# Fourier mixing and a long convolution on one core: u and K side by side in one tile of the second transform stage

## Chip, cores and metric

The kernel runs on one core of one Trainium2 chip. The metric is the time of one execution on the device in microseconds, the median of several runs. A profile of one further execution shows what each engine did.

## What is computed

The output has two halves side by side. The first is a Fourier mixing layer on x (2048 x 512) with given real and imaginary matrices. The second is a state-space layer: a kernel K of 2048 taps for each of 512 channels is built from exponentials, u (2048 x 512) is convolved with it by transforms of length 4096, and u times a skip factor is added.

```python
# first half
a = einsum("bsd,ed->bse", x, dft_hid_re)
b = einsum("bsd,ed->bse", x, dft_hid_im)
y = einsum("ts,bse->bte", dft_seq_re, a) - einsum("ts,bse->bte", dft_seq_im, b)
# second half
P = exp((A * dt[:, None])[:, :, None] * pos[None, None, :])
K = 2.0 * einsum("dn,dnl->dl", C, P).real
Kf, Uf = rfft(K, 2 * L), rfft(u_t, 2 * L)
y = irfft(Uf * Kf[None], 2 * L)[:, :, :L]
y = y.transpose(0, 2, 1) + u * D_skip
```

## The kernel before

Two programs share the engines. `Fnet` does the first half: twelve groups of outputs, each made of four accumulators of 128 x 512, and every step of a group multiplies three products of split operands (high times high, high times low, low times high) in `matmuls`, line 304. These 1,920 matmuls are the stream that fills TensorE. Its operands are loaded into `raw` (line 272, on SP's queue) and split by ScalarE (line 184) and VectorE (line 188) into `hi` and `lo`; four `raw` buffers and three split pairs are in turn.

`Ssm` does the second half in pieces that are put in between. `tables1` and `tables2` build factors of the exponentials on VectorE and ScalarE (lines 543 to 572). `taps` (line 739) multiplies two such tables into the taps of K for 32 channels, 16 times. `stage1_k` (line 769) and `stage1_u` (line 812) do the first stage of the transform, of K eight times and of u eight times, and store the result in device memory (`xk`, `xu`). `product` does the rest for one of 16 groups: four parts h of 128 channels by four ranges q of frequencies. It multiplies the first-stage result of u and of K by the second-stage pieces `w2` (line 890), copies both spectra from the accumulator banks with ScalarE (line 903), multiplies them on VectorE (lines 906 to 919), and applies the first piece of the inverse (line 926) into `zs`. `inverse` (line 972) ends a part.

The order of all instructions is fixed before the run: generators yield an engine and an estimated duration, an event or a semaphore of buffers, and the class `Plan` simulates them and writes the instructions out in the order in which they would start. Each engine then works through its own list in that order. Almost all loads and stores are issued by one queue, SP's.

The load of one group's first-stage result is `load_spectrum`: two DMAs, for r = 0 and 1, from line 863, into a tile `xt_u` for u and another, `xt_k`, for K, of 128 x 2 x 4 x 128 floats each. The two names have counts of free buffers, `b.xts["u"]` and `b.xts["k"]`: one buffer for the parts h = 0 to 2, two for h = 3. `spectra` runs once for u and once for K, waits for a buffer and spawns the load. `products` waits for both loads, takes two pairs of accumulator banks and spawns `product`. In it, r, then u or K, then the real or imaginary output c, then the strip xx of 32 output rows and the half g of the contracted rows are looped over, one matmul each:

```python
nc.tensor.matmul(got[r][1][32 * xx:32 * xx + 32, g, o:o + PART],
                 self.w2[rows, 2 * q + r, xx, 32 * c:32 * c + 32], xt[rows, r, xx],
                 start=True, stop=True, tile_position=(64 * g, 32 * xx))
```

A matmul contracts 64 rows into 32 outputs for 128 columns, and takes one of eight tiles of the array (two by row, four by column). All operands are 32-bit floats; `PART` is 128. In one accumulator bank lie, 128 columns each, u real, u imaginary, K real and K imaginary.

Early in the run, before any spectrum is loaded, `stage1_u` uses the same two buffers for its inputs: piece k of u goes to `xt_u` for even k and to `xt_k` for odd k (line 806).

Of the kernel before, what the change touches and what calls it, by code (L numbers as in the profile page):

```python
# [8 lines left out]
F32 = mybir.dt.float32  # L9
# [7 lines left out]
SEQ, DM, NS = 2048, 512, 128  # L17
PART = DM // 4
# [127 lines left out]
def act(cols):  # L146
    return 0.09 + cols * 0.00085


def dve(cols, rate=1.0):  # L150
    return (62 + cols / rate) / 960


def load(kb):
    return max(0.55, kb / 330)
# [210 lines left out]
class Ssm:  # L366
# [423 lines left out]
    def spectrum_u(self):  # L790

        self.uleft = 16
        yield self.const_ev
        b = self.sets[0]
        yield b.zls
        self.xu_sb, self.xus = b.pool.tile([128, 2, 2, DM], F32, name="zl", bufs=b.n), Sem(2)
        for k in range(8):
            name = "uk"[k % 2]
            yield self.sets[0].xts[name]
            self.plan.spawn(self.stage1_u(k, name), 1)  # L800

    def stage1_u(self, k, name):
        nc, b = self.nc, self.sets[0]
        u = b.pool.tile([128, 2, DM], F32, name=f"xt_{name}")
        yield "dma", load(512)
        nc.sync.dma_start(u, self.uG[:, 2 * k:2 * k + 2])
        got = yield from self.banks(2)
        yield "pe", 1.82
        for m in range(2):
            for r in range(2):  # L810
                rows = slice(64 * r, 64 * r + 64)
                nc.tensor.matmul(got[m][1][:, r], self.f1u[rows], u[rows, m], start=True, stop=True,  # L812
                                 tile_position=(64 * r, 0))
        self.plan.put(b.xts[name])
        for m in range(2):
            n = 2 * k + m
            sem = b.zbs if n % 3 == 2 else self.xus
            yield sem
            x = b.pool.tile([128, 2, DM], F32, name="z", bufs=b.n) if n % 3 == 2 else self.xu_sb[:, n % 3]
            for r in range(2):  # L820
                yield "act", act(512)
                nc.scalar.activation(x[:, r], got[m][1][:, r], AF.Copy)
            self.give(got[m][0])
            self.plan.spawn(self.store_u(x, 2 * k + m, sem), 1)
# [32 lines left out]
                self.plan.spawn(self.load_spectrum(b, name, h, q, view), 1)  # L857

    def load_spectrum(self, b, name, h, q, view):
        xt = self.xt[name, h, q] = b.pool.tile([128, 2, 4, PART], F32, name=f"xt_{name}", bufs=b.n)  # L860
        yield "dma", load(512)
        for r in range(2):
            self.nc.sync.dma_start(xt[:, r], view[2 * q + r])
        self.plan.set(self.xt_ev[name, h, q])

    def products(self):
# [12 lines left out]
    def product(self, b, h, q, got, done):  # L879
        nc, v, a = self.nc, self.nc.vector, self.nc.scalar  # L880
        uk = b.pool.tile([128, 2, 2, 2, 2, PART], F32, name="uk", bufs=b.n)
        yield "pe", 1.86
        for r in range(2):
            for n, name in enumerate("uk"):
                xt = self.xt[name, h, q]
                for c in range(2):
                    for xx in range(4):
                        for g in range(2):
                            rows, o = slice(64 * g, 64 * g + 64), (2 * n + c) * PART
                            nc.tensor.matmul(got[r][1][32 * xx:32 * xx + 32, g, o:o + PART],  # L890
                                             self.w2[rows, 2 * q + r, xx, 32 * c:32 * c + 32], xt[rows, r, xx],
                                             start=True, stop=True, tile_position=(64 * g, 32 * xx))
        for name in "uk":
            self.plan.put(b.xts[name])
        self.plan.set(done)
        u, t = uk[:, :, :, 0], uk[:, :, :, 1]
        yield b.zbs
        P = b.pool.tile([128, 2, 2, 2, PART], F32, name="z", bufs=b.n)
        left, ready = [2], Event()

        def half(r, k, p):
            yield "act", act(1024)
            a.activation(uk[:, r].rearrange("p g n c d -> p g (n c d)"), p, AF.Copy)  # L903
            self.give(k)
            yield "dve", dve(512)
            v.tensor_tensor(P[:, r], t[:, r], u[:, r], op=OP.mult)  # L906
            yield "dve", dve(512), *APART
            v.tensor_tensor(t[:, r], t[:, r], u[:, r, :, ::-1], op=OP.mult)  # L908
            left[0] -= 1
            if not left[0]:  # L910
                self.plan.set(ready)
        for r in range(2):
            self.plan.spawn(half(r, *got[r]), 1)
        yield ready
        yield "dve", dve(512)
        v.tensor_tensor(u[:, :, :, 0], P[:, :, :, 0], P[:, :, :, 1], op=OP.subtract)
        self.plan.put(b.zbs)
        yield "dve", dve(512), *APART
        v.tensor_tensor(t[:, :, :, 0], t[:, :, :, 0], t[:, :, :, 1], op=OP.add)

        def run(got):
            for c, Y in enumerate((u, t)):
                for g in range(2):
                    for xx in range(4):
                        rows = slice(32 * xx, 32 * xx + 32)
                        nc.tensor.matmul(got[xx // 2][1][64 * g:64 * g + 64, xx % 2, :2 * PART], self.ia[rows, c],  # L926
                                         Y[rows, :, g, 0], start=c == 0, stop=c == 1, tile_position=(32 * xx, 64 * g))
        w = Joined(self, run)
        if self.taps_left:
            self.waiting.append(w)  # L930
            yield w
        if w.got is None:
            got = yield from self.banks(2)
            yield "pe", 0.95
            w.run(got, False)
        self.plan.put(b.uks)
        yield b.zbs
        z = b.pool.tile([128, 2, 4, PART], F32, name="z", bufs=b.n)
        for n, (k, p) in enumerate(w.got):
            yield "act", act(512)  # L940
            a.activation(z[:, :, 2 * n:2 * n + 2].rearrange("p r x d -> p x r d"),  # L941
                         p[:, :, :2 * PART].rearrange("p x (r d) -> p x r d", r=2), AF.Copy)
            w.leave(k)
        view = self.zs[h].rearrange("(q x g) c l d -> q (g c l) x d", q=8, x=4)
        yield "dma", load(512)
        for r in range(2):
            nc.sync.dma_start(view[2 * q + r], z[:, r])
        self.plan.put(b.zbs)
        self.left[h] -= 1
        if not self.left[h]:  # L950
            self.plan.set(self.zs_ev[h])
# [108 lines left out]
```

## Time and profile before

| what | us |
|---|---|
| median of 3 runs | 593.32 (591.82 to 596.59) |
| the profiled execution | 595.39 |
| its span, from the first instruction to the last | 593.6 |
| granted TensorE clock in it, share of full speed | 0.997 |

The profile counts each float32 matmul of the second half as two records and each matmul of the stream as one; each record has a weight load (PEld) of its own, which may overlap matmuls. A group row gives line, engine, operation, output and inputs, shapes and count, then busy time and the mean of one in ns, then the idle time of the engine before it and what ended that. The chain of waits is followed back from the last instruction to whatever released each step; "issue" in it is time in which the engine waited for nothing that the profile shows. In a listing by tile, a row has shortest/median/longest duration in ns and the first and last start in us, then the tile of the array (rows*columns) and the moving operand. In a list of waits the three numbers are us in total, times and the longest. A row of a DMA queue has packets, MB and share of the 16 engines' time; a row of DMA issues has the count, KB of each and median us to landing.

### The profile page before, as it was taken

What the parts mean: (1) busy time and instruction counts of PE and PEld (TensorE: products, weight loads), DVE (VectorE), ACT (ScalarE), POOL (GpSimd) and SP (SyncE); (2) the same over time, 40 slices, a digit from 0 to 9 for tenths busy, and PEclk for the clock granted to TensorE, in tenths of its full rate; (3) what the DMA queues carried; (4) which work ended last, traced back from release to release, by engine and by line L of the source; (5) the groups of instructions that cost most, each with busy time, mean ns of one, the idle gap of its engine ahead of it and who ended that gap; (6) DMA issues with size and microseconds to landing.
All of it is one profiled execution on the core that took longest, in us unless ns stands there. A gap on an engine that the chain in (4) does not pass through costs nothing.

```text
span 593.6 us, 16944 instructions
## 1 busy us (share of the span) xinstructions
PE 583.3 (98%) x6982; PEld 451.1 (76%) x6982; DVE 496.6 (84%) x883; ACT 382.2 (64%) x745; POOL 4.6 (1%) x12
## 2 busy tenths in 40 slices
PE   8999999999999999999899999999999999999997
PEld 6767668778788777876687788778776877877785
DVE  7977989999999999999899999999999944245420
ACT  5789884947586587758474876677764635353622
POOL 0000000000000000000000000000000000000000
PEclk9999999999999999999899999999999999999999
DMA  8999996363493359456947783569787744998674
GB/s 270 332 365 334 319 337 198 107 178 94 122 274 100 105 162 280 118 150 174 253 130 228 196 258 116 146 159 287 232 275 209 239 118 144 282 340 267 197 249 142
DMA packets 141247, 125.97 MB, mean 212 GB/s; under 512 B 46193, under 2 KB 106353, under 8 KB 140913
## 3 DMA queue, kind: packets, MB, share of 16 engines
q1 hardware_dynamic: 140880, 124.48, 69.0%
q8 instruction: 55, 0.90, 0.6%
q10 hardware_dynamic: 288, 0.39, 0.2%
q14 instruction: 24, 0.19, 0.1%
HBM read 82.12 MB, written 42.73 MB: 210 GB/s over the span
## 4 chain that ended last, share of the span: by engine, by line
PE 85%; DVE 6%; DMA 3%; issue 2%; ACT 2%; SPq 1%; DVEq 0%; ACTq 0%
PE acc L304 66%; PE f L739 5%; PE f L890 4%; PE f L926 3%; PE f L812 3%; PE f L769 2%; PE f L972 2%; DVE prod L543 2%; DMA zl<-zs 1%; DVE lo L188 1%; DVE t L552 1%; DMA par<-par_dram 1%; DMA uk<-in_x 1%; ACT hi L184 0%; ACT y L327 0%
## 5 line engine op out<-in xcount | busy, mean ns | idle before, releaser
L304 PE MATMUL acc<-hi,x_hi 128*128 128x512 f32 x640 | 257.7, 403 | 0.4 <-ACT x_hi L184 0.2
L304 PE MATMUL acc<-hi,x_lo 128*128 128x512 f32 x640 | 250.6, 392 | 0.3 <-issue 0.2
L304 PE MATMUL acc<-lo,x_hi 128*128 128x512 f32 x640 | 250.5, 391 | 0.2 <-DVE lo L188 0.2
L543 DVE TENSOR_TENSOR prod<-t,cs 128x1024 f32<-128x1024 f32 (+4 forms) x192 | 163.5, 870 | 3.1 <-ACT t L681 0.9
L188 DVE TENSOR_TENSOR lo<-raw,hi 128x512 fp32r<-128x512 f32 x160 | 109.1, 686 | 62.0 <-ACT hi L184 56.2
L184 ACT ACTIVATE hi<-raw 128x512 fp32r<-128x512 f32 x160 | 100.5, 629 | 92.4 <-PE acc L304 68.7
L304 PEld LDWEIGHTS acc<-hi,x_hi 128*128 128x128 f32 x640 | 120.5, 188 | 45.4 <-issue 17.8
L304 PEld LDWEIGHTS acc<-hi,x_lo 128*128 128x128 f32 x640 | 120.7, 189 | 27.1 <-issue 0.7
L304 PEld LDWEIGHTS acc<-lo,x_hi 128*128 128x128 f32 x640 | 120.6, 189 | 24.0 <-DVE lo L188 0.9
L552 DVE TENSOR_TENSOR t<-prod 128x512 f32<-128x512 f32 (+4 forms) x192 | 94.5, 512 | 1.1
L559 ACT ACTIVATE square<-t 128x256 f32<-128x256 f32 (+1 forms) x64 | 36.6, 571 | 21.6 <-DVE t L552 20.2
L327 ACT ACTIVATE y<-acc 128x512 f32<-128x512 f32 x47 | 27.9, 596 | 13.1 <-PE acc L304 9.6
L739 PEld LDWEIGHTS f<-t,t 128*32 128x32 f32 x2048 | 29.5, 110 | 8.0 <-issue 5.7
L903 ACT ACTIVATE uk<-f 128x1024 f32<-128x1024 f32 x32 | 32.1, 1016 | 4.9 <-PE f L890 3.6
L739 PE MATMUL f<-t,t 128*32 128x64 f32 x2048 | 32.4, 220 | 1.7 <-issue 1.7
L906 DVE TENSOR_TENSOR z<-uk 128x512 f32<-128x512 f32 x32 | 22.0, 686 | 8.4 <-ACT uk L903 4.7
L572 DVE TENSOR_TENSOR t<-square 128x128 f32<-128x128 f32 (+1 forms) x64 | 24.7, 386 | 0.3 <-ACT square L559 0.3
L941 ACT ACTIVATE z<-f 128x512 f32<-128x512 f32 x32 | 17.6, 596 | 11.3 <-PE f L739 5.8
L890 PE MATMUL f<-xt_k,w 64*32 64x128 f32 x1024 | 22.7, 271 | 1.9 <-issue 1.9
L618 ACT ACTIVATE cs<-cs 128x352 f32<-128x352 f32 x32 | 15.9, 537 | 11.7 <-DVE cs L613 11.7
L908 DVE TENSOR_TENSOR uk<-uk 128x512 f32<-128x512 f32 x32 | 22.1, 690 | 0.8
L566 DVE SCALAR_TENSOR_TENSOR t<-t 128x128 f32<-128x128 f32 (+2 forms) x48 | 22.4, 466 | 0.4
(85 smaller groups left out, 440.7 us busy)
## 6 DMA issues: line engine op xcount, KB each, us to landing
raw<-in_sT SPq DMA_DIRECT2D x127, 256.0 KB, 3.4
p<-y SPq DMA_DIRECT2D x32, 256.0 KB, 3.9
xt_u<-xu SPq DMA_DIRECT2D x32, 256.0 KB, 5.1
xk<-xk_sb SPq DMA_DIRECT2D x32, 256.0 KB, 4.0
xt_k<-xk SPq DMA_DIRECT2D x32, 256.0 KB, 5.5
zs<-z SPq DMA_DIRECT2D x32, 256.0 KB, 3.7
zl<-zs SPq DMA_DIRECT2D x16, 512.0 KB, 6.3
raw<-p SPq DMA_DIRECT2D x32, 256.0 KB, 4.2
```

The source lines that it names most:

```text
L184: self.nc.scalar.activation(hi, src, AF.Copy)
L188: self.nc.vector.tensor_tensor(lo, src, hi.bitcast(F32), op=OP.subtract)
L304: nc.tensor.matmul(acc[d], l[:, cols], r, start=k == 0 and n == 0, stop=k == len(items) - 1 and n == 2)
L327: self.nc.scalar.activation(y, ps, AF.Copy, scale=-1.0 if g[2] == 1 else 1.0)
L543: self.nc.vector.tensor_tensor(p.rearrange("p k d c m -> p k (d c) m"), src.rearrange("p d c l -> p (d c) l")[:, None, :, rows].to_broadca ...
L552: self.nc.vector.tensor_tensor(dst[:, :, :, rows], p[:, 0], p[:, 1, :, ::-1], op=OP.add)
L559: self.nc.scalar.activation(sq, t[:, :, :, m // 2:m], AF.Square)
L566: self.nc.vector.scalar_tensor_tensor(t[:, :, 1, m:2 * m:2], t[:, :, 0, m // 2:m], 2.0, t[:, :, 1, m // 2:m], op0=OP.mult, op1=OP.mult)
L572: self.nc.vector.tensor_tensor(t[:, :, 0, m:2 * m:2], box[0][:, :, 0], box[0][:, :, 1], op=OP.subtract)
L739: nc.tensor.matmul(ps[32 * j:32 * j + 32, i], t1[:, d, c], t2[:, d, c], start=c == 0, stop=c == 1, tile_position=(0, 32 * j))
L890: nc.tensor.matmul(got[r][1][32 * xx:32 * xx + 32, g, o:o + PART], self.w2[rows, 2 * q + r, xx, 32 * c:32 * c + 32], xt[rows, r, xx], star ...
L903: a.activation(uk[:, r].rearrange("p g n c d -> p g (n c d)"), p, AF.Copy)
```

## The change

The two tiles become one, `xt`, of 128 x 2 x 4 x 2 x 128 floats: for each r and strip xx, the 128 columns of u and next to them the 128 of K. The first of the two loads of a group takes the tile, and each load fills its own 128 columns of every 256. `product` loses the loop over u and K: one matmul takes 256 columns, and its output goes to two strips of the bank, 128 columns apart, so that the bank holds the same as before. The two counts of free buffers stay. `stage1_u` uses the two halves of one such tile for even and odd k. The estimate for the planner, 1.86 us for a product, is not changed.

```diff
         for k in range(8):
             name = "uk"[k % 2]
-            yield self.sets[0].xts[name]
+            yield b.xts[name]
+            if not k:
+                self.u_sb = b.pool.tile([128, 2, 2, DM], F32, name="xt", bufs=b.n)
             self.plan.spawn(self.stage1_u(k, name), 1)
...
-        u = b.pool.tile([128, 2, DM], F32, name=f"xt_{name}")
+        u = self.u_sb[:, k % 2]
...
     def load_spectrum(self, b, name, h, q, view):
-        xt = self.xt[name, h, q] = b.pool.tile([128, 2, 4, PART], F32, name=f"xt_{name}", bufs=b.n)
+        if (h, q) not in self.xt:
+            self.xt[h, q] = b.pool.tile([128, 2, 4, 2, PART], F32, name="xt", bufs=b.n)
+        xt = self.xt[h, q]
         yield "dma", load(512)
         for r in range(2):
-            self.nc.sync.dma_start(xt[:, r], view[2 * q + r])
+            self.nc.sync.dma_start(xt[:, r, :, "uk".index(name)], view[2 * q + r])
...
+        xt = self.xt[h, q]
         for r in range(2):
-            for n, name in enumerate("uk"):
-                xt = self.xt[name, h, q]
-                for c in range(2):
-                    for xx in range(4):
-                        for g in range(2):
-                            rows, o = slice(64 * g, 64 * g + 64), (2 * n + c) * PART
-                            nc.tensor.matmul(got[r][1][32 * xx:32 * xx + 32, g, o:o + PART],
-                                             self.w2[rows, 2 * q + r, xx, 32 * c:32 * c + 32], xt[rows, r, xx],
-                                             start=True, stop=True, tile_position=(64 * g, 32 * xx))
+            for c in range(2):
+                for xx in range(4):
+                    for g in range(2):
+                        rows = slice(64 * g, 64 * g + 64)
+                        both = got[r][1][32 * xx:32 * xx + 32, g].rearrange("p (n c d) -> p n c d", n=2, c=2)
+                        nc.tensor.matmul(both[:, :, c], self.w2[rows, 2 * q + r, xx, 32 * c:32 * c + 32],
+                                         xt[rows, r, xx], start=True, stop=True, tile_position=(64 * g, 32 * xx))
```

## The prediction

> **What bounds the kernel now.** I read the page first: shares of the engines, then the chain of waits.
>
> ```profile
> span 593.6 us, 16944 instructions
> PE 583.3 (98%) x6982; PEld 451.1 (76%) x6982; DVE 496.6 (84%) x883; ACT 382.2 (64%) x745; POOL 4.6 (1%) x12
> PE 85%; DVE 6%; DMA 3%; issue 2%; ACT 2%; SPq 1%; DVEq 0%; ACTq 0%
> PE acc L304 66%; PE f L739 5%; PE f L890 4%; PE f L926 3%; PE f L812 3%; PE f L769 2%; PE f L972 2%; DVE prod L543 2%; DMA zl<-zs 1%; DVE lo L188 1%; DVE t L552 1%; DMA par<-par_dram 1%; DMA uk<-in_x 1%; ACT hi L184 0%; ACT y L327 0%
> ```
>
> TensorE is busy 98% of the span and carries 85% of the chain. Two thirds of the chain is the stream of the first part (L304), which the change leaves alone. The transform that changes is L890, 4%. So the question is what one block at L890 costs, and what ends around it.
>
> The merged chain shows each block with its time (start, us, what) and the group rows show how many records a block has.
>
> ```profile
> 27.97 1.92 PE f L812 x8
> 83.17 1.92 PE f L739 x128
> 105.71 1.93 PE f L769 x16
> 169.87 1.96 PE f L890 x128
> 303.48 1.90 PE f L972 x32
> 535.87 1.05 PE f L926 x32
> ...
> L890 PE MATMUL f<-xt_u,w x1024: 267/269/295, 169.8 to 556.2; 64*32 64x128 f32 x171
> L890 PE MATMUL f<-xt_k,w x1024: 268/269/293, 170.3 to 556.6; 64*32 64x128 f32 x171
> L926 PE MATMUL f<-uk,ia x512: 374/374/426, 198.6 to 563.9; 32*64 32x256 f32 x171
> L739 PE MATMUL f<-t,t x2048: 219/219/244, 83.1 to 485.2; 128*32 128x64 f32 x187
> ```
>
> A product has 64 calls of matmul in the code and 128 records in its block: each float32 matmul is two records. With 2,048 records at L890, there are 16 such blocks.
>
> **Does a block pay for instructions or for columns?** Give each record a weight: its columns times the share of the 128x128 array that its tile takes. L890: 128 records x 128 columns x (64x32)/(128x128) = 2,048. L739: 128 x 64 x 1/4 = 2,048. L926: 32 x 256 x 1/8 = 1,024. By their forms in the listing below, L812 (64x128 tiles), L769 (32x128) and L972 (128x64) come to 8 x 512 x 1/2, 16 x 512 x 1/4 and 32 x 128 x 1/2: 2,048 each.
>
> ```profile
> L972 PE MATMUL f<-zl,ib x256: 272/273/323, 303.4 to 583.2; 128*64 128x128 f32 x128
> L769 PE MATMUL f<-ks,f1k x128: 587/587/692, 105.6 to 498.0; 32*128 32x512 f32 x128
> L812 PE MATMUL f<-xt_u,f1u x32: 589/589/693, 27.9 to 74.8; 64*128 64x512 f32 x32
> ```
>
> Every block of weight 2,048 takes 1.90 to 1.96 us, whether it has 8 records or 128; the one of weight 1,024 takes 1.05. So a block costs about 0.85 ns per unit of weight ((1.92 - 1.05)/1,024) and 0.18 us for its ends. It pays for columns, and the tiles side by side are already full.
>
> **Term 1, the block itself.** The change makes it 64 records of 256 columns on 64x32 tiles: 64 x 256 x 1/8 = 2,048, as before. Its nearest row is L926, which is already 256 columns wide, eight tiles in turn: doubling its inner part gives 1.05 + 0.87 = 1.92 us; L972 allows 1.90. So a block gains 0.04 to 0.06 us, about what the narrow form loses to its many weight loads. I take 0.05: 16 x 0.05 = 0.8 us. On the chain L890 has 4.4% of 593.6 = 26 us, some 13 of 16 blocks, so 0.6 to 0.7 us reach the end. I take 0.6, with 0 and 1.0 as ends.
>
> A rule of the Trainium skill would make much more of it: TensorEngine Tiling (Array Packing), section Instruction Overhead, gives each matmul about 60 cycles of overhead, so that one of 1 column takes as long as one of 60. At the 2.4 GHz of its page TensorE: Matmul & The Clock Gate that is an estimated 25 ns, 1.6 us for the 64 records saved in a block, 26 us over 16 blocks. This trace disagrees, as 128 records end in 1.96 us, 15 ns each, and 8 records take 1.92.
>
> **Term 2, the supply of instructions.** "issue" in the chain is time in which nothing shown was awaited. Three such pieces lie inside TensorE's blocks:
>
> ```profile
> 287.86 1.93 PE f L890 x125
> 289.79 1.92 issue
> 291.70 0.41 PE f L890 x3
> ...
> 456.80 1.70 PE f L739 x112
> 458.50 1.07 issue
> ...
> 482.58 1.91 PE f L739 x123
> 484.48 0.62 issue
> ```
>
> Together 1.92 + 1.07 + 0.62 = 3.6 us. TensorE stops near the end of a block whose other records run at full pace. The queues show what runs then; the first row is for the whole span, the others for 289.0 to 291.7, 456.8 to 459.6 and 482.4 to 485.1 us.
>
> ```profile
> q8 instruction: 55, 0.90, 0.6%
> ...
> q8 instruction: 1, 0.02, 2.1%
> ...
> q8 instruction: 1, 0.02, 2.1%
> ...
> q8 instruction: 1, 0.02, 2.8%
> ```
>
> 0.90 MB in 55 packets is 16.4 KB each. TensorE's 2 x 6,982 records over 55 are 254 per packet, so this queue feeds TensorE some 256 instructions at a time. Each stop has one such packet in it, and each comes in a stretch where an inverse piece (32 records and as many weight loads, 64 instructions), a block of taps (256), four pieces of the stream (24) and a product (256) run through 600 instructions in some 8 us. I read the stops as TensorE running out of instructions.
>
> The Trainium skill has the same blocks (Runtime: NRT & Kernel Launch, section Instruction fetch mechanics: 16 KiB, 256 instructions) and says that the fetch is mostly hidden. The size agrees with 16.4 KB; that it is hidden does not fit the three stops here. By that rule term 2 would be nothing, and the forecast 592.7.
>
> The change takes 64 matmul records and 64 weight loads out of every product: 2,048 instructions, 8 packets of 55, and the run of 600 becomes 470. The stop inside L890 (1.92) should go. The two in L739 come before the product, and depend on where the 256 boundary falls; it moves by half a packet with each product, so they may go, stay or turn up elsewhere. I count half: 0.85. Sum 2.8 us, ends 0 (all come back) and 3.6 (all go). What replaces a stop: the stream goes on at once, as L304 has lost nearly nothing to its operands.
>
> ```profile
> L304 PE MATMUL acc<-hi,x_hi 128*128 128x512 f32 x640 | 257.7, 403 | 0.4 <-ACT x_hi L184 0.2
> ```
>
> **Edits at no cost.** The shape of the planner's work is the same: the waits at xts, the 1.86 us for a product and the events keep their places, so the order of instructions stays, on SP's queue too. The loads of u and K stay 32 each of 256 KB. Their destination becomes pieces of 512 bytes, but the source (128 floats of one row) is in such pieces already. They land 5 us after issue, and TensorE shows no wait for them:
>
> ```profile
> raw<-in_sT SPq DMA_DIRECT2D x127, 256.0 KB, 3.4
> ...
> xt_u<-xu SPq DMA_DIRECT2D x32, 256.0 KB, 5.1
> xt_k<-xk SPq DMA_DIRECT2D x32, 256.0 KB, 5.5
> ...
> SPq L863 <- PE f L890: 2.2, 4, 1.0
> SPq L272 <- DVE lo L188: 165.1, 85, 4.8
> ```
>
> What does move: u's next load waited for the last matmul of u, and now waits for the last of the product, a quarter block (0.5 us) later. SP's issues wait there 4 times now (2.2 us), so 2 us of waiting at most are added on a queue that idles 165 us for buffers of the stream (L272); without that cover it would cost these 2 us. The first matmul now needs K's first half too, a quarter block earlier. ScalarE's eviction still starts at each half.
>
> **Sum.** The profiled execution took 595.39 us (span 593.6). Minus 0.6 and 2.8 gives 592.0. It is 2.1 us above the median of the runs, 593.32, and some of the stops may be what it has more than the others; so against the median I take two thirds of term 2, 1.9: 593.32 - 0.6 - 1.9 = 590.8. **Forecast 591 us.**
>
> **Rivals.**
> *Matmuls are bound by their issue.* Then the block falls to near half: 16 x 0.85 = 13.6 us less, 580. For it: 2,048 records fewer. Against: L812 and L739, 8 and 128 records, both 1.92. Chance 3%.
> *The supply of instructions costs more than the three stops.* Unseen waits of the same kind at block ends, and the DVE-bound stretch near 250 us starting earlier, would double term 2 to 5.6 on top of 0.6: 587. Chance 13%.
> *The fetch only moves.* Stops return elsewhere, term 1 alone: 592 to 595. Chance 21%.
> *Slower: the shared tile ties the two loads together.* The price comes from these rows (SP's timeline, then the two splits of a load) and from the landing of raw above:
>
> ```profile
> 510.09 1.05 SPq L863 DMA_DIRECT2D xt_u<-xu x2
> ...
> L188 DVE TENSOR_TENSOR lo<-raw,hi 128x512 fp32r<-128x512 f32 x160 | 109.1, 686 | 62.0 <-ACT hi L184 56.2
> L184 ACT ACTIVATE hi<-raw 128x512 fp32r<-128x512 f32 x160 | 100.5, 629 | 92.4 <-PE acc L304 68.7
> ```
>
> If K's load is held until u's into the same tile has landed, SP stands 5.1 us less the 1 us of u's two issues, 4 us, in each of 16 products, and the stream's loads (L272) stand behind it. The stream has three split buffers of 4 x 0.685 = 2.7 us each by the planner, 8 us less 3.4 us of landing and 1.3 of splitting: 3.4 us of cover, so some 0.6 us show per product if all is well, up to 4 where ScalarE and VectorE are late. 16 x 1 = 16 us, 609. It decides if one wait of K's load on u's is there at all. Against: the pieces are disjoint, and a like pair runs free now. L566 writes every second element beside what L559 on ScalarE reads from the same table, and is not shown waiting for it, while L572, which needs L559's result, is:
>
> ```profile
> L572 DVE TENSOR_TENSOR t<-square 128x128 f32<-128x128 f32 (+1 forms) x64 | 24.7, 386 | 0.3 <-ACT square L559 0.3
> L566 DVE SCALAR_TENSOR_TENSOR t<-t 128x128 f32<-128x128 f32 (+2 forms) x48 | 22.4, 466 | 0.4
> ```
>
> Chance 7%.
> *Writing two strips 128 columns apart at half pace.* No row writes a bank like this; it would double the inner part: 16 x 1.74 = 28, 621. Chance 3%.
>
> **Chances and range.** The forecast's own case (588 to 592.5) has the remaining 53%. A change below 1%, 5.9 us, is about what a measurement of this kernel can tell from none. Faster by more: the first rival and most of the second, 0.15. Slower by more: the two slow ones and a little for an unlucky phase, 0.11. Same 0.74. The runs before spread from 591.82 to 596.59, so the range reaches from 587 (all stops gone and a little more) to 597 (nothing gained, a slow reading); the rivals at 580, 609 and 621 stay outside, with about 15% between them and the edges.
>
> **What would show it.** Records of L890: 1,024 in place of 2,048, of 64x256. A block of 1.90 to 1.92 us: term 1; 1.0 would be the first rival, 3.7 the last. Packets on the instruction queue: 47. Pieces of issue inside L890: none, and fewer than 3.6 us in all for matmuls into f. SP waiting at L863 for DMA xt_u: the tied loads. The forecast is wrong if the block changes by more than 0.1 us, or SP's queue shows a new wait.

## The result and the profile after

The changed kernel takes 590.44 us (median of 8 runs, 589.31 to 591.15) against 593.57 us for the kernel before, run beside it (8 runs, 591.82 to 596.59). The ratio is 0.9945, with a 95% interval of 0.9924 to 0.9966: 3.1 us or 0.55% less, clear of noise and below 1%. The profiled execution took 590.22 us, its span 588.4.

The page of the changed kernel: span, engines, the queue of instructions, and the row of the matmul that was widened (busy us, mean ns, then idle time before it).

```profile
span 588.4 us, 14902 instructions
PE 580.2 (99%) x5958; PEld 439.7 (75%) x5958; DVE 496.5 (84%) x883; ACT 380.8 (65%) x745; POOL 4.7 (1%) x12
q8 instruction: 47, 0.77, 0.5%
L894 PE MATMUL f<-xt,w 64*32 64x256 f32 x1024 | 31.3, 379 | 0.0
```

The records are 1,024 of 256 columns, where 2,048 of 128 were, and the packets of instructions 47, where 55 were. The chain of waits of the changed kernel (start, us, what) has one block of the product and the two stops of TensorE that are left:

```profile
286.15 1.31 issue
...
370.86 0.57 issue
371.43 0.31 PE f L739 x6
...
401.98 1.89 PE f L894 x64
```

The same block in the chain of the kernel before:

```profile
404.33 1.96 PE f L890 x128
```

The block is 0.07 us shorter, as all 16 are: 1.1 us, a little less on the path, since two of the 16 lie in the stretch from 226 to 276 us that VectorE bounds. The stops were 1.92 + 1.07 + 0.62 = 3.6 us and are 1.31 + 0.57 = 1.9 us, at other places: one in the stream ahead of a product, one in a block of taps, none in the product.

That makes 2.8 us, but the two profiled spans differ by 5.2. The windows of the kernel before show what else it lost, behind its longest stop (columns: us of the window, busy us and records of each engine, granted clock, DMA share, GB/s):

```profile
291.00:293.00 2.00, 1.30 (x7) 0.95 (x8) 1.97 (x8) 0.00 (x0) 0.00 (x0) 1.00 0.96 298
293.00:296.50 3.50, 3.50 (x11) 2.69 (x10) 1.13 (x3) 0.92 (x3) 0.00 (x0) 0.51 0.89 224
296.50:300.00 3.50, 3.50 (x17) 2.89 (x16) 2.93 (x5) 2.11 (x6) 0.00 (x0) 1.00 0.80 277
```

For 3.4 us the granted clock was half, and the matmuls of the stream started 0.43 us apart instead of 0.23: eight ran where 15 would have, about 1.6 us lost. Its waits for a load of `zl` (0.5 us at 527 us) are gone too. This brings the sum to 4.9 of the 5.2 us. That profiled execution was one of the long ones, 595.39 us against a median of 593.57. The changed kernel has no stretch of half clock in its profile:

```profile
core 0: 588.4 us, clock 1.000
```

The order of instructions on VectorE, ScalarE, GpSimd and SP's queue is the same in both kernels, entry by entry, if waits for semaphores are left aside, and so is the order of the blocks on TensorE. SP's waits for the product, 2.2 us in 4 times before, are now:

```profile
SPq L867 <- PE f L894: 4.2, 6, 1.2
```

These are the 2 us foreseen for u's next load, on a queue that waits far more elsewhere.

### The profile page after: what moved, and what is told of

The parts are those of the page before. It is cut to its first block, busy times and chain, and to the rows that moved or that the text cites. A ratio compares the mean times of both kernels' runs of the same rounds, so it can differ in the third digit from the quotient of the medians.

```text
span 588.4 us, 14902 instructions
## 1 busy us (share of the span) xinstructions
PE 580.2 (99%) x5958; PEld 439.7 (75%) x5958; DVE 496.5 (84%) x883; ACT 380.8 (65%) x745; POOL 4.7 (1%) x12
## 4 chain that ended last, share of the span: by engine, by line
PE 69%; DVE 21%; issue 4%; DMA 3%; ACT 2%; SPq 1%; DVEq 0%; ACTq 0%
PE acc L304 52%; DVE prod L543 7%; DVE lo L188 4%; DVE t L552 4%; PE f L894 4%; PE f L739 3%; PE f L814 3%; PE f L975 3%; PE f L929 2%; PE f L769 2%; DMA xt<-xk 1%; DVE t L572 1%; DMA raw<-in_sT 1%; DVE t L566 1%; DVE cs L613 1%
## 5 line engine op out<-in xcount | busy, mean ns | idle before, releaser
L739 PEld LDWEIGHTS f<-t,t 128*32 128x32 f32 x2048 | 29.4, 110 | 6.8 <-issue 4.1
L739 PE MATMUL f<-t,t 128*32 128x64 f32 x2048 | 32.2, 220 | 0.6 <-issue 0.6
L894 PE MATMUL f<-xt,w 64*32 64x256 f32 x1024 | 31.3, 379 | 0.0
L894 PEld LDWEIGHTS f<-xt,w 64*32 64x32 f32 x1024 | 18.4, 106 | 10.9 <-issue 4.6
```

The costliest lines, as they stand in the source:

```text
L739: nc.tensor.matmul(ps[32 * j:32 * j + 32, i], t1[:, d, c], t2[:, d, c], start=c == 0, stop=c == 1, tile_position=(0, 32 * j))
L894: nc.tensor.matmul(both[:, :, c], self.w2[rows, 2 * q + r, xx, 32 * c:32 * c + 32], xt[rows, r, xx], start=True, stop=True, tile_position= ...
```

## The experiments

**1. The tile without the wide matmuls.** The joint tile and its loads stay, the product goes back to 64 calls of 128 columns.

```diff
         for r in range(2):
-            for c in range(2):
+            for n in range(2):
+                for c in range(2):
...
-                        nc.tensor.matmul(both[:, :, c], self.w2[rows, 2 * q + r, xx, 32 * c:32 * c + 32],
-                                         xt[rows, r, xx], start=True, stop=True, tile_position=(64 * g, 32 * xx))
+                            nc.tensor.matmul(both[:, n, c], self.w2[rows, 2 * q + r, xx, 32 * c:32 * c + 32],
+                                             xt[rows, r, xx, n], start=True, stop=True,
+                                             tile_position=(64 * g, 32 * xx))
```

> The joint tile and its two loads as in the change, but the matmuls narrow again (64 of 128 columns per product). Theory (the block pays for columns, and TensorE runs out of instructions after it): nothing of the gain is left, ratio 1.00 (0.998 to 1.003, about 593.6 us), L890's block back at 1.96 us, 55 packets on the instruction queue, stops inside blocks of some 3 to 4 us in all. Rival (the gain comes from the joint tile, its loads and waits): the gain stays, ratio 0.995, about 590.5 us. Second rival (the joint tile has a hidden cost that the wide matmuls outweigh): slower than before, ratio above 1.003.

Measured: 593.46 us, ratio 0.9992 (0.9975 to 1.0008), 55 packets. The chain of waits of this kernel at its stops:

```profile
287.69 1.93 PE f L895 x125
289.61 1.92 issue
291.54 0.41 PE f L895 x3
...
457.15 1.70 PE f L739 x112
458.86 0.92 issue
...
482.75 1.90 PE f L739 x123
484.65 0.41 issue
```

These are the three stops of the kernel before, after the same number of records of the same blocks (125, 112 and 123). Nothing of the gain belongs to the tile, its loads or its waits; they cost nothing that shows either.

**2. Matmuls of 64 columns.** In the kernel before, each matmul of the product is cut in two.

```diff
                 for c in range(2):
+                    for s in (0, 64):
...
-                            rows, o = slice(64 * g, 64 * g + 64), (2 * n + c) * PART
-                            nc.tensor.matmul(got[r][1][32 * xx:32 * xx + 32, g, o:o + PART],
+                                rows, o = slice(64 * g, 64 * g + 64), (2 * n + c) * PART + s
+                                nc.tensor.matmul(got[r][1][32 * xx:32 * xx + 32, g, o:o + 64],
...
+                                                 xt[rows, r, xx, s:s + 64],
...
```

> The kernel before with every matmul of the product cut into two of 64 columns: the same columns, 256 records and 256 weight loads per block, 4,096 instructions more, 71 packets. Theory (instructions come 256 at a time, and two packets in a row were 3.6 to 5.3 us apart): a block of 512 instructions cannot end in 2 us; each product stops for at least one packet, 2 to 4 us, and many stops are long enough for the half clock: 16 x 2 to 5 us, 625 to 675 us. Rival (columns alone count, the three stops were chance of another kind): 592 to 596 us, blocks of 1.9 to 2.1 us. Rival (each record has a price of its issue, 15 ns as in the narrow block): blocks of 3.7 us evenly filled, without stops inside, 16 x 1.8 = 28 us more, 622 us.

Measured: 665.33 us, one run, beside 593.77 for the kernel before. Its waits of TensorE, one product in its chain, its queue of instructions and its clock:

```profile
PE f L891 <- issue: 42.9, 17, 5.2
...
433.51 1.86 PE f L891 x119
435.37 3.23 issue
438.60 1.09 PE f L891 x63
...
q8 instruction: 71, 1.16, 0.7%
...
core 0: 663.5 us, clock 0.976
```

The same work with twice the instructions costs 71.5 us. TensorE stops 17 times at this line for 42.9 us, where it stopped once for 1.9. With the stop taken out, the block takes 1.86 + 1.09 = 2.95 us in place of 1.96: 16 us in all. (The chain lists 119 + 63 of its 256 records; the others are hidden behind these.) The clock of 0.976 leaves out 16 us of full clock over the span, where 0.997 left out 2: 14 more. 41 + 16 + 14 is the 71, an estimate, since the parts overlap a little. Both plain rivals fall: the stops make up most of it. But the block without its stop is not free of its instructions either: at 64 columns a record takes 2.95 us / 256 = 11.5 ns, so on tiles of 64x32 the rule that a block pays for columns alone ends between 128 and 64 columns. On tiles twice that size it still holds at 64: the block of taps (L739, 128x32) takes 1.92 us for its 128 records, 15 ns each.

**3 and 4. Another phase of the packets.** If the stops come where a packet of 256 instructions ends at a bad place, then adding instructions far ahead must move them, with nothing else changed. Both kernels got 128 instructions more in the warm-up.

```diff
             self.nc.tensor.matmul(ps[:, :256], z[:, :128], z[:, 256:], start=n == 0, stop=n == 2)
+        for n in range(32):
+            self.nc.tensor.matmul(ps[:, :16], z[:, :128], z[:, 256:272], start=True, stop=True)
```

> The kernel before with 32 small matmuls of 16 columns added to the warm-up at the start, before the first operands are there: 128 instructions, half a packet, more ahead of everything; no other change. Theory: the same 3.6 us kind of stops, but at other blocks, since the ends of the packets fall elsewhere; the time moves by up to 4 us either way (589.5 to 597), with 55 or 56 packets. Rival (the stops belong to these places: data, waits or loads): stops again inside L890 after 287 us and L739 after 456 and 482 us, and the time of before within 1 us.

> The changed kernel with the same 32 small matmuls in the warm-up. Theory: its stops (1.3 us in the stream after 286 us and 0.6 us in L739 after 370 us) move to other places; blocks of L894 stay at 1.90 us; 588 to 593 us. Rival (the changed kernel has no stops but by its order of work): the same places, 590.4 within 0.5 us.

Measured: 609.52 us (ratio 1.0283, 1.0251 to 1.0315) and 606.03 us (1.0208, 1.0174 to 1.0242). The expected times were missed, since the added matmuls were not small in time; the chain of the padded kernel before shows them:

```profile
4.50 13.47 PE acc L206 x64
17.97 24.14 PE acc L306 x96
```

They took 13.5 us, 0.21 us a record, and held up the stream. For the times the two runs say nothing, but the places did move. With the 14 us taken off, the padded kernel before stops at 371 and 397 us in blocks of taps and for under 1 us at three other places (in the stream, in a product and in an inverse), and no longer at 289, 458 and 484; the padded changed kernel stops at 396, and no longer at 286 and 370. Its chain there:

```profile
408.23 1.85 PE f L741 x121
410.07 1.92 issue
411.99 0.32 PE f L741 x7
```

So a rule could be read off the profiles so far. Count TensorE's instructions from the start, weight loads and waits for semaphores included, and take the count at which a block of taps begins modulo 256. With 194 to 225, it stopped in 6 of 7 cases in the profiles of the two kernels and of experiments 3 and 4, and at no other offset. (The expectation below speaks of five profiles; with experiment 1, which repeats the kernel before, it is 8 of 9.)

**5 to 8. The rule put to the test.** This time the pad is small matmuls on four tiles in turn, ahead of the warm-up: 16 of them for 64 instructions, 48 for 192.

```diff
         yield "pe", 2.6
+        for n in range(16):
+            j = 32 * (n % 4)
+            self.nc.tensor.matmul(ps[j:j + 32, 256:272], z[:, :32], z[:, 256:272], start=True, stop=True,
+                                  tile_position=(0, j))
         for n in range(3):
```

> The changed kernel with 16 small matmuls on four tiles in turn ahead of its warm-up: 64 instructions, a quarter packet, more. In the five profiles so far a taps block that begins 194 to 225 instructions after a multiple of 256 stopped in 6 of 7 cases, and no other taps block did. Theory: 64 more put one of this kernel's later taps blocks (the one near 225 us, in the stretch bound by VectorE) into that window and take the one near 369 us out of it: at most 1 us of stops on the path, 589 to 591.5 us with up to 0.5 us for the added matmuls. Rival (stops do not depend on the count of instructions): the stops at 286 and 370 us stay.

> The same with 48 small matmuls, 192 instructions. Theory: the taps blocks near 177, 199, 255 and 424 us come into the window: three or four stops of 0.6 to 2 us, slower than the pad of 64 by 2 to 5 us beyond the 0.9 us that 32 more small matmuls may cost: 592 to 597 us. Rival: as the pad of 64, within 1 us.

> The kernel before with 64 instructions more at the start. Theory: the taps blocks near 177, 200, 226, 255 and 427 us come into the window (two of them in the stretch bound by VectorE), those near 457 and 483 us leave it: stops at 177, 200 and 427 us, none in L890 after 288 us; 593.5 to 598 us. Rival: the three stops stay at 288, 457 and 483 us.

> The kernel before with 192 instructions more. Theory: only the taps block near 341 us comes into the window, so fewer stops than before: 591 to 594 us with up to 1.3 us of cost at the start, and faster than the pad of 64 by 1 to 5 us. This is what is left of the gain if the stops go but the blocks stay narrow. Rival: as the pad of 64 or slower by the 0.9 us of the added matmuls.

| kernel | us | ratio to before (95%) | taps blocks at offset 194 to 229 (after an inverse piece), and whether they stopped |
|---|---|---|---|
| changed, pad 64 | 589.60 | 0.9922 (0.9897 to 0.9947) | 201 stops |
| changed, pad 192 | 590.95 | 0.9957 (0.9939 to 0.9975) | 199 and 213 stop; 223 and 228 do not |
| before, pad 64 | 593.58 | 0.9990 (0.9967 to 1.0013) | 198, 199 and 200 stop; 219 does not |
| before, pad 192 | 595.74 | 1.0032 (1.0008 to 1.0056) | 220 stops |

The chain of the changed kernel with a pad of 192 at one of its two stops, 422.77 us, offset 213:

```profile
422.77 1.81 PE f L743 x118
424.58 1.54 issue
426.12 0.41 PE f L743 x10
```

The old stops were gone, but for one: in the kernel before with a pad of 64, the product after 288 us still stopped, for 0.35 us, and 32 records (64 instructions) earlier than before, after 93 in place of 125:

```profile
289.13 1.49 PE f L894 x93
290.62 0.35 issue
```

Of the 11 blocks of taps named ahead, seven stopped, by their count alone; the other four began at 219 to 223. Over the nine profiles of experiments 1 and 3 to 8 and of the two kernels, all 12 taps blocks at 194 to 213 stopped, 3 of 9 at 219 to 229 (after an inverse piece), and none elsewhere.

The traces show a simpler rule behind this. In all twelve profiles, those of experiments 2, 9 and 10 included, there are 51 stops of TensorE of over 0.15 us that the profile puts down to "issue", in taps, products, inverses and the stream. Each time, the matmul that comes late has 193 or 194 instructions ahead of it, modulo 256, by the same count; no wait that the profile puts down to another engine or to a load falls there. So TensorE stops at one fixed place in each packet's worth of 256 instructions, and the offset of a block tells how much of it has run by then: 237 instructions or more, nearly a whole packet, where the block begins at 194 to 213. Most packets pass that place without a stop: 50 of 54 in the kernel before, where a fourth stop, of 0.2 us, lies in the stream.

The expectations of time held for the pads of 64, and failed for those of 192. In the changed kernel, two of the four blocks named began at 223 and did not stop, so it was 1.35 us slower than the pad of 64, not 2 to 5. In the kernel before, the rule for the taps left out the other blocks; its chain with a pad of 192 stops behind and inside the product:

```profile
315.89 1.96 PE f L894 x128
317.85 0.43 PE acc L308
318.28 1.12 issue
...
430.80 0.83 PE f L894 x45
431.64 1.26 issue
432.89 1.50 PE f L894 x82
...
463.84 0.89 PE acc L308 x3
464.73 1.08 issue
```

Three stops, 3.5 us, all at or just behind a product of 256 instructions: this kernel became slower, by a ratio of 1.0032, with a pad that left the taps one stop of 0.6 us. In no profile with wide matmuls did a product stop inside its block.

**9 and 10. Is the changed kernel with the pad of 64 the better one?** Both once more, on one chip.

> The changed kernel once more, beside the next one on the same chip. Theory: 0.9945 of before within 0.002, with the stops at 286 and 370 us again.

> The changed kernel with 64 small instructions at the start once more. Theory: its one stop lies in the stretch bound by VectorE, so it saves the two of the changed kernel (1.3 and 0.6 us of issue on the chain) and pays 0.4 us at the start: 0.7 to 1.5 us faster than the changed kernel, ratio to before 0.992 to 0.994. Rival (the stops that the profile shows are gone in most executions): as the changed kernel or 0.4 us slower.

Measured: 590.26 us (ratio 0.9941, 0.9921 to 0.9961) and 589.46 us (0.9928, 0.9906 to 0.9950). The one stop of the padded kernel is the expected one at 228 us, and the repeated changed kernel has its two again:

```profile
228.43 1.35 issue
```

```profile
286.26 0.73 issue
...
370.36 0.70 issue
```

The median with the pad was 0.8 us lower here, and as much lower in experiment 5 against the first result, but the intervals overlap, so that a gain is likely and not settled.

## Why the prediction was right

The forecast was 591 us, 2.3 us below the median it was worked from, and the measured medians are 590.44 and 590.26.

**What bounds the kernel, and columns against instructions.** Right: twice the columns in half the records left the block at 1.89 us, near the 1.90 to 1.92 that L972 and L926 gave, and not at half. Experiment 2 shows where the argument ends: at 64 columns the block itself grows by 1.0 us.

**Term 1** was slightly too small: 0.05 us a block was taken and 0.07 measured, 1.1 us over 16 blocks where 0.8 stood before the share of the chain.

**Term 2**, the supply of instructions, was right in kind and about right in size. The stop inside L890 went, those in L739 went, and two others came: 1.7 us saved where 2.8 had been taken for the profiled execution and 1.9 for the median. The half counted for the stops in L739 was a guess on where packets end, and came to nothing: 1.7 us went there and 1.9 came back at other places. That the cause is the number of instructions, and not the product's data or loads, was an inference from the packets; experiments 1 and 3 to 8 show it, since the stops stay when the tile changes and the count doesn't, and move when the count changes and nothing else does, always to the same place in the count. What exactly a packet waits for was not tried.

**What the prediction left out** is the half clock behind the longest stop, 1.6 us of the profiled execution. It stood on the page, as one 8 in the row of the clock. This fits the profiled spans, which moved by 5.2 us, and the medians, which moved by 3.1: of the 47 runs of the kernel before beside the experiments, 11 have a clock of 0.997 or less, with a median of 594.9 us, and the other 36 one of 593.5. Taking the sum against the profile, and then only two thirds of term 2 against the median, came out close by luck, for a partly wrong reason: the surplus of the profiled run was the clock more than the stops.

**The edits at no cost** cost nothing: experiment 1 at 0.9992. The tied loads did not come about, as no wait of K's load on u's shows, and loads land after 4.4 and 5.0 us, where it was 5.1 and 5.5. Strips 128 columns apart are written at full pace.

**Two rules beside the rows.** The overhead of about 60 cycles a matmul (the Trainium skill, TensorEngine Tiling (Array Packing), section Instruction Overhead) would have given an estimated 26 us; the 16 blocks gave 1.1. By the Trainium skill's Runtime: NRT & Kernel Launch, section Instruction fetch mechanics, blocks of 256 instructions are fetched mostly out of sight; the size agrees (254 instructions a packet), but experiment 2 has 42.9 us of stops in sight.

## What to carry to other kernels

Small matmuls on tiles side by side can be bound by their columns and still cost time by their number: here TensorE was fed some 256 instructions at a time (11,916 in 47 packets), and runs of several hundred short ones emptied it, which the chain of waits shows as "issue" inside a block. Widen matmuls where such runs are densest, and do not expect more than these stops and a few hundredths of a microsecond per block. Since the stops depend on where packets end, any edit that changes the number of TensorE's instructions moves them, and with them the time by up to two microseconds here; count to the places where they can fall, and look at them, before a difference of that size is put down to the edit's own purpose.

## What the runs showed of the hardware that was not expected

A stop of TensorE of about 2.2 us from start to start was followed by 3.4 us of half clock, in the kernel before, in experiment 1 and in experiment 4 (stop rows of 1.92 us); in these profiles and those of experiments 3 and 5 to 10, the stops with rows of 1.72 us and less were not. The clock's cost, 1.6 us, is near that of the stop itself. But the length does not decide it alone. In experiment 2, seven of the eight stops of 2.4 us and more have half clock at their end or within 1.1 us of it, but the one of 3.23 us shown above has full clock behind it (the 1.00 in its row), as have those of 1.99, 2.12 and 2.13 us:

```profile
438.60:442.00 3.40, 3.40 (x98) 2.91 (x98) 0.71 (x2) 1.38 (x3) 0.00 (x0) 1.00 0.88 290
```

What else decides was not tried.

The pad of experiments 3 and 4, 64 records of 16 columns on the whole array, took 13.5 us: 0.21 us each, with weight loads as long as this:

```profile
L206 PEld LDWEIGHTS acc<-y x64: 333/333/337, 3.9 to 17.5; 128*128 128x128 f32 x64
```

The stream's weight loads of the same size take 331 to 333 ns at the start of the kernel before too, and 188 ns later. The first matmuls of the stream behind the pad took 0.63 us each until 22.6 us, as those at the half clock do. The profile prints a granted clock of 1.00 there, but the trace's record of the clock begins only at 22.6 us (at 6.3 us in the kernel before), so this 1.00 is not a measurement. The pads of experiments 5 to 8, with loads of 32 columns on four tiles in turn, are much cheaper. The 96 records of the pad of 192, at the start too, take 15 ns each:

```profile
1.58 1.48 PE L205 MATMUL acc<-y 128*32 128x16 f32 x96 [1.58 <-DVE y L201]
```

They moved the first block of taps by no more than 0.7 us. So where a pad for phase is wanted, small loads on several tiles cost a fraction of loads of the whole array; which of the two, size or number of tiles, makes it so was not tried apart.
